# A retention layer and a rational feed-forward on one core: other turns for the first two blocks, sign halfwords on GpSimd, zero products in TensorE's waits

## The chip, the cores and the metric

The kernel runs on one core of a Trainium2 chip. The metric is the device time of one execution in microseconds (us), median of several runs; lower is better. The engines are TensorE (PE; its weight loads are listed as PEld), VectorE (DVE), ScalarE (ACT), GpSimd (POOL) and SyncE (SP), which here only issues DMAs. Each engine works through its own queue in the order written; semaphores make it wait for the others. SBUF is the on-chip memory, PSUM the eight banks (b0 to b7) into which TensorE writes.

## The reference

```
state = gamma[h] * state + k_t (x) v_t           # per batch (4) and head (8), 768 steps, 64 x 64 states
y_t   = (q_t . state) / 8
x     = y as 3072 tokens x 512
h = x @ w_in                                      # 512 -> 2048
P = a0 + a1*h + a2*h^2 + a3*h^3
Q = 1 + |b0|*|h| + |b1|*h^2
out = (P / (Q + 1e-6)) @ w_out                    # 2048 -> 512
```

All inputs are float32, but for `w_in` and `w_out`, which arrive as float64 and must be brought to float32 on the chip.

## The kernel before

**Blocks and slots.** The 768 steps are cut into 6 chunks of 128. Chunk n of the four batches makes block n: 512 tokens. The feed-forward of a block is cut into 16 slices of 128 hidden columns; one slice of one block is a *slot*, 96 in all, numbered k = 0 to 95. The first 32 slots are those of blocks 0 and 1, since the weights are decoded while they run: eight slices of block 0, eight of block 1, the other eight of block 0, the other eight of block 1. Blocks 2 to 5 follow one after the other.

**A slot.** Numbers are split into two parts of lower precision, so each product is three: 12 matmuls of 128x512.
- first product (L665, PSUM tile `ph`): w x, with x in two parts `xh` and `xl`;
- then A1 |h| (L718), A2 scale and offset (L727 on ScalarE, or L723 on GpSimd), A3 (L733), P1 product (GpSimd, L738), D1 (VectorE, L741 and L742), A4 reciprocal (ScalarE, L747 and L750), D2 (VectorE, L754 to L756), A6 cast to `gh` (ScalarE, L762), P2 rest `gl` (GpSimd, L766);
- second product (L680, step O, PSUM tile `po`, banks b4 to b7), which is summed over the slots of a group. Behind a group's last slot four copies (L804) take the sums out; those of the first groups of blocks 0 and 1 go to memory, and are fetched and added (L801) behind the second.

**Decoding a weight tile.** There are 32 tiles of 512 KB (16 of each matrix). `low` (ScalarE, L625) makes the low bits from one byte of each float64, `high` (ScalarE, L629) the high part, VectorE *joins* them in two instructions (L635 shifts and ors the parts, L638 ors the sign bit in), `split` (ScalarE, L644) casts the first part `w[:, 0]`, `rest` (GpSimd, L647) the second. Tile `t`, into which low writes, has two buffers; it is free again after rest.

**Retention.** Chunk c of batch b is *batch* i = 4c + b of 24. It loads kT, qT, v, k (and q2T, v2 for c > 0), GpSimd scales k (L439), TensorE makes scores (S: L312, or L350 and L358), VectorE masks them (L480), TensorE makes the values (R: L318 and L326, or L376), and ScalarE and VectorE write `xh` and `xl` (L569, L573). Batches 0 to 3 make block 0's x; batches 4 to 7, that of block 1, run among the first slots.

**What sets the order.** `Plan` in the kernel orders all steps ahead of time. Each step has engines, a cost, what it follows, the buffers it takes, and a rank, from `RANKS` by batch or tile, or the slot's number, plus an offset by kind (`OFFSETS`). The plan goes through time, and on the engine that can begin first it takes the step of lowest rank that can begin within `LOOK`; A2 goes to whichever of its engines the plan finds (up to slot `SHARED`). `LOADS` ranks the loads. What comes out is the fixed queue of each engine. While TensorE would wait for more than 600 ns ahead of the first first product, `emit` puts in products of a zero tile (L893, tile `idle`).

Of the kernel before, what the change touches and what calls it, by code (L numbers as in the profile page):

```python
# [9 lines left out]
U32 = mybir.dt.uint32  # L10
U8 = mybir.dt.uint8
# [13 lines left out]
COLD = 2600, 3200  # L25
# [19 lines left out]
class Plan:  # L45
# [84 lines left out]
    def order(self, emit):  # L130

        then = {}
        for x in self.steps:
            x.waits = len(x.after)
            for a, _ in x.after:
                then.setdefault(a, []).append(x)
        open_ = []

        def enter(x):
            x.known = 0  # L140
            for a, early in x.after:
                x.known = max(x.known, a.start if early is None else a.end - early + WAKE)
            open_.append(x)

        for x in self.steps:
            if not x.waits:
                enter(x)
        left = len(self.steps)
        while left:
            self.claims = []  # L150
            for x in open_:
                for b in x.takes:
                    if b.options and len(b.options()) == 1:
                        self.claims.append((x, frozenset(b.options()[0])))
            by_engine = {}
            for x in open_:
                t = self.ready(x)
                if t is None:
                    continue
                for e in x.engines:  # L160
# [12 lines left out]
            gap = start - self.free.get(e, 0)  # L173
            self.commit(x, e, start)
            emit(x, e, gap)
            open_.remove(x)
# [8 lines left out]
def tile_retention_rational_ffn(  # L185
# [29 lines left out]
    HF = NF // 2  # L215
# [20 lines left out]
    zeros = ff.tile([P, DM], F32, name="o", bufs=BUFS["o"]).bitcast(BF16)[:, :TB]  # L236
# [171 lines left out]
    def attention(i, rank, load_rank, gate):  # L408
# [38 lines left out]
        pa, aT = Buffer("psum", pairs), [Buffer("aT") for _ in range(2)]  # L447
# [164 lines left out]
    def decode(m, f, rank, load_rank):  # L612
# [8 lines left out]

        def low(_):
            cell["t"] = ff.tile([P, DM], U32, name="t", bufs=BUFS["t"])
            byte = cell["raw"].rearrange("p m w -> p (m w)").bitcast(U8)[:, 3::8]
            nc.scalar.activation(cell["t"], byte, AF.Identity, bias=lcon[:, 0:1], scale=1.0 / 32)  # L625
# [25 lines left out]
        J = step(("DVE",), (1300, 1385), join, [L, U], rank, uses=[t, u], kind="join")  # L651
# [33 lines left out]
    stores, sums, halves = {}, {}, {}  # L685
# [7 lines left out]
    def slot(k, n, f, first, final):  # L693
# [100 lines left out]
        part = None if n >= 2 else f // HF  # L794
        for tt in range(SPB):
            o = Buffer("o") if part != 1 else sums[n, tt][0]

            def copy(engine, tt=tt, o=o):
                if part == 1:
                    o_ = cell["o", tt] = sums[n, tt][1]["tile"]  # L800
# [5 lines left out]
            def write(_, tt=tt):  # L806
                dst = out[(tt * C + n) * P : (tt * C + n + 1) * P, :]
                if part == 0:
                    dst = halves[n, tt] = dram.tile([P, DM], F32, name=f"half{n}_{tt}")
# [3 lines left out]
            after = [(O, early)] + ([sums[n, tt][2]] if part == 1 else [])  # L813
            engines = ("DVE",) if part == 1 else (("ACT",), ("DVE",))[tt % 2]
            Y = step(
                engines, {"ACT": (480, 590), "DVE": (600, 685)}, copy, after, k + 3.6,
                [] if part == 1 else [o], [po] + ([o] if part == 1 else []),
            )
            W = step(("SP",), (ISSUE, 700), write, [Y], k, uses=[o])
            stores[n, part, tt] = W  # L820

    def load_sums(n, gate):
        for tt in range(SPB):
            o = Buffer("o")
            x, cell = load(
                lambda: ff.tile([P, DM], F32, name="o", bufs=BUFS["o"]), lambda tt=tt: halves[n, tt],
                4 * P * DM, 0.0, [o], after=[(gate, None), stores[n, 0, tt]],
# [5 lines left out]
    order = [(n, f) for h in range(2) for n in range(2) for f in range(h * HF, (h + 1) * HF)]  # L833
    order += [(n, f) for n in range(2, NB) for f in range(NF)]
    starts = {}
    for n in range(1, NB):
        end = order.index((n, 0))
        begin = {1: 0, 2: 3 * HF}.get(n, end - NF)
# [3 lines left out]
    with tc.manual_schedule(  # L842
# [25 lines left out]
        for k, (n, f) in enumerate(order):  # L868
# [17 lines left out]
        def emit(x, engine, gap):  # L886

            nonlocal idle
            if engine == "PE" and not begun(1) and gap > 600:
                if idle is None:  # L890
                    idle = ps.tile([P, TB], F32, name="idle", tag="b1")
                for _ in range(min(10, int(gap / 430))):
                    nc.tensor.matmul(idle, zeros[:, :P], zeros, start=True, stop=True)  # L893
            x.run(engine)

# [22 lines left out]
}  # L918
RANKS = {
# [123 lines left out]
```

## Time and profile before

| | |
|---|---|
| median of 3 runs | 621.59 us (620.14 to 621.78) |
| the profiled execution | 622.29 us, of which 620.5 us is the span from the first to the last instruction |
| busy share of the span | PE 97%, DVE 72%, ACT 68%, POOL 56% |
| mean granted TensorE clock | 0.989 |
| DMA | 59.44 MB; HBM read 50.21 MB, written 8.39 MB |

Busy is the time in which at least one instruction of an engine runs. Matmuls are pipelined, so that PE counts as busy while products follow one another; products of zeros count as busy too. The granted clock is the share of full speed that TensorE got. A row of the timeline merges instructions alike in a row: start, duration, engine, line, operation, tiles (out<-in), shapes, count, and in brackets the idle time ahead of it and what ended that.

### The profile page before, as it was taken

Reading aid. Unit: us, or ns where it says so; the run is one execution under the profiler, and the core shown is the slowest. Engines: PE = TensorE matmul, PEld = TensorE weight load, DVE = VectorE, ACT = ScalarE, POOL = GpSimd, SP = SyncE. Lnnn points to the kernel's source line nnn. Section 1 sums busy time; section 2 is a strip of 40 time slices with the busy share of each in tenths; the row PEclk is TensorE's granted clock in tenths of the full one; section 3 lists DMA queues with packets and bytes.
Section 4 is the critical chain, followed back from the end, with each engine's and each line's share of the span. In section 5 each row is a group of like instructions: output and inputs, shape, how many; then the busy total and the mean of one; then the engine's idle time right before and its main releaser. Section 6 shows DMA issues by size and latency. Waiting matters only on the chain.

```text
span 620.5 us, 13030 instructions
## 1 busy us (share of the span) xinstructions
PE 601.5 (97%) x5155; PEld 485.9 (78%) x5155; DVE 449.1 (72%) x743; ACT 421.6 (68%) x700; POOL 347.0 (56%) x303
## 2 busy tenths in 40 slices
PE   8858999999999999999999999999999999999997
PEld 4736877888887888887888888888888888888885
DVE  3689788999979867767766776667766666666662
ACT  1687779999965555565666766666666666776772
POOL 2387677998867675654544545444444444444442
PEclk9968999999999999999999999999999999999999
DMA  8999631003024330224411222112311100100001
GB/s 304 411 414 414 233 86 69 1 1 135 1 86 155 120 120 17 69 69 121 130 43 52 103 73 66 35 52 69 120 52 36 34 1 0 61 9 1 1 0 69
DMA packets 30733, 59.44 MB, mean 96 GB/s; under 512 B 3536, under 2 KB 8912, under 8 KB 30672
## 3 DMA queue, kind: packets, MB, share of 16 engines
q1 hardware_dynamic: 30672, 58.62, 26.8%
q8 instruction: 40, 0.66, 0.4%
q14 instruction: 21, 0.17, 0.1%
HBM read 50.21 MB, written 8.39 MB: 94 GB/s over the span
## 4 chain that ended last, share of the span: by engine, by line
PE 88%; POOL 2%; DVE 1%; ACT 1%; issue 1%; POOLq 0%; DVEq 0%; ACTq 0%
PE po L680 41%; PE ph L665 41%; PE px L376 3%; PE pa L350 2%; PE pa L358 1%; POOL w L647 1%; POOL gl L766 1%; POOL q L738 0%; ACT ph L750 0%; POOL s L723 0%; ACT s L747 0%; DVE q L754 0%; DVE p L756 0%; DVE ph L755 0%; ACT gh L762 0%
## 5 line engine op out<-in xcount | busy, mean ns | idle before, releaser
L665 PE MATMUL ph<-xh,w 128*128 128x512 f32 (+2 forms) x776 | 209.0, 392 | 3.4 <-DVE p L756 2.3
L680 PE MATMUL po<-w,gh 128*128 128x512 f32 x768 | 203.4, 397 | 6.2 <-ACT gh L762 5.3
L738 POOL TENSOR_TENSOR q<-q,s 128x512 f32<-128x512 f32 x96 | 124.2, 1294 | 147.0 <-ACT s L727 144.3
L680 PEld LDWEIGHTS po<-w,gh 128*128 128x128 f32 x768 | 143.0, 189 | 37.6 <-ACT gh L762 5.4
L665 PEld LDWEIGHTS ph<-xh,w 128*128 128x128 f32 x776 | 144.2, 189 | 35.3 <-DVE p L756 4.1
L766 POOL TENSOR_TENSOR gl<-p,gh 128x512 fp32r<-128x512 f32 x96 | 124.1, 1292 | 27.5 <-ACT gh L762 18.0
L754 DVE SCALAR_TENSOR_TENSOR q<-q,small,ph 128x512 f32<-128x512 f32 x96 | 71.6, 745 | 93.7 <-ACT ph L750 91.8
L718 ACT ACTIVATE q<-ph 128x512 f32<-128x512 f32 x96 | 57.3, 596 | 87.7 <-PE ph L665 87.3
L680 PE MATMUL po<-w,gl 128*128 128x512 f32 x384 | 111.6, 392 | 0.9 <-POOL gl L766 0.9
L665 PE MATMUL ph<-xl,w 128*128 128x512 f32 (+2 forms) x388 | 104.0, 390 | 0.0
L747 ACT ACTIVATE s<-q,small 128x512 f32<-128x512 f32 x96 | 69.5, 724 | 49.2 <-POOL q L738 49.2
L741 DVE TENSOR_TENSOR p<-ph,p 128x512 f32<-128x512 f32 x96 | 65.8, 685 | 30.2 <-ACT p L733 29.1
L680 PEld LDWEIGHTS po<-w,gl 128*128 128x128 f32 x384 | 72.6, 189 | 16.8 <-POOL gl L766 1.7
L665 PEld LDWEIGHTS ph<-xl,w 128*128 128x128 f32 x388 | 73.2, 189 | 15.3
L733 ACT ACTIVATE p<-ph,small 128x512 f32<-128x512 f32 x96 | 74.3, 774 | 2.1 <-POOL gl L766 2.1
L742 DVE SCALAR_TENSOR_TENSOR p<-p,small,ph 128x512 f32<-128x512 f32 x96 | 71.8, 748 | 3.4
L762 ACT CAST gh<-p 128x512 fp32r<-128x512 f32 x96 | 59.2, 617 | 20.1 <-PE po L680 13.0
L755 DVE SCALAR_TENSOR_TENSOR ph<-p,small,ph 128x512 f32<-128x512 f32 x96 | 71.9, 749 | 0.0
L756 DVE SCALAR_TENSOR_TENSOR p<-q,ph 128x512 f32<-128x512 f32 x96 | 65.9, 686 | 3.3
L750 ACT ACTIVATE ph<-s 128x512 f32<-128x512 f32 x96 | 57.8, 602 | 3.7
L647 POOL TENSOR_TENSOR w<-t,w 128x512 fp32r<-128x512 f32 x32 | 41.2, 1293 | 19.8 <-ACT w L644 10.8
L727 ACT ACTIVATE s<-q,small 128x512 f32<-128x512 f32 x61 | 49.7, 814 | 0.3
(53 smaller groups left out, 445.8 us busy)
## 6 DMA issues: line engine op xcount, KB each, us to landing
raw<-in_w_in SPq DMA_DIRECT2D x16, 512.0 KB, 7.6
raw<-in_w_out SPq DMA_DIRECT2D x16, 512.0 KB, 7.8
kT<-in_kT SPq DMA_DIRECT2D x24, 256.0 KB, 3.3
qT<-in_qT SPq DMA_DIRECT2D x24, 256.0 KB, 3.2
v<-in_v SPq DMA_DIRECT2D x24, 256.0 KB, 3.9
k<-in_k SPq DMA_DIRECT2D x24, 256.0 KB, 3.6
out<-o SPq DMA_DIRECT2D x24, 256.0 KB, 2.6
q2T<-in_q2T SPq DMA_DIRECT2D x20, 128.0 KB, 3.2
```

Of the source, the lines that this page charges most:

```text
L665: nc.tensor.matmul(cell["ph"][:, t0:t1], w[0, f][:, part, kt * P : (kt + 1) * P], x[:, kt, t0:t1], start=(i == 0), stop=(i == 3 * NP - 1),)
L680: nc.tensor.matmul(o_tiles[n][tt], g_[:, tt * P : (tt + 1) * P], w[1, f][:, part], start=(first and m == 0), stop=(last and m == 2),)
L733: nc.scalar.activation(cell["p"], cell["ph"], AF.Identity, bias=par_sb[:, 2:3], scale=par_sb[:, 3:4])
L738: nc.gpsimd.tensor_mul(cell["q"], cell["q"], cell["s"])
L741: nc.vector.tensor_mul(cell["p"], cell["ph"], cell["p"])
L742: nc.vector.scalar_tensor_tensor(cell["p"], cell["p"], par_sb[:, 1:2], cell["ph"], ALU.add, ALU.mult)
L747: nc.scalar.activation(cell["s"], cell["q"], AF.Abs_reciprocal_sqrt, bias=qcon[:, 0:1])
L754: nc.vector.scalar_tensor_tensor(q_, q_, qcon[:, 0:1], ph_, ALU.add, ALU.mult)
L755: nc.vector.scalar_tensor_tensor(ph_, p_, par_sb[:, 0:1], ph_, ALU.add, ALU.mult)
L756: nc.vector.scalar_tensor_tensor(p_, q_, 2.0, ph_, ALU.subtract, ALU.mult, reverse0=True)
L762: nc.scalar.copy(cell["gh"], cell["p"])
L766: nc.gpsimd.tensor_sub(cell["gl"], cell["p"], cell["gh"].bitcast(F32))
```

## The change

- `GROUPS = (0, 10, 16)`: the first 32 slots go in groups of 10, 10, 6 and 6 instead of four of 8.
- For 14 of the 32 weight tiles (`SIGNS`) GpSimd makes the upper halfword of `t`, which holds only the sign, with one compare-and-multiply on 16-bit elements; `low` then writes the lower halfword alone, and one VectorE instruction joins (L638 goes).
- Products of zeros (`fill`, 37 in all; 23 before) now also stand in waits of over 900 ns behind the first first product, into the bank that the next step takes or, as a sum of zeros, into the open sum of a second product. The zeros have a tile of their own.
- `t` has three buffers. The masked scores of batches 0 to 3 take buffers of `o`. The last of the four copies is ScalarE's and the first VectorE's.
- The plan's constants (`COLD`, `HOLD`, `LOOK`, `EARLY`, `SHARED`), ranks, offsets and load ranks are others; the plan looks only at the six loads of lowest rank.

```
-COLD = 2600, 3200
+COLD = 2600, 1000
...
+    def fill(bank, start):
+        for _ in range(spare[0]):
+            nc.tensor.matmul(
+                bank, zeros, zeros.unsqueeze(1).broadcast_to([P, TB // P, P]), start=start, stop=start,
+                skip_group_check=True,
+            )
+        spare[0] = 0
...
+        aside = (m, f) in SIGNS
         def low(_):
...
-            nc.scalar.activation(cell["t"], byte, AF.Identity, bias=lcon[:, 0:1], scale=1.0 / 32)
+            to = cell["t"].bitcast(U16)[:, ::2] if aside else cell["t"]
+            nc.scalar.activation(to, byte, AF.Identity, bias=lcon[:, 0:1], scale=1.0 / 32)
+
+        def sign(_):
+            words = cell["raw"].rearrange("p m w -> p (m w)").bitcast(U16)[:, 3::4]
+            nc.gpsimd.tensor_scalar(
+                cell["t"].bitcast(U16)[:, 1::2], words, 32768.0, 32768.0, op0=ALU.is_ge, op1=ALU.mult
+            )
...
         def join(_):
             u_, t_ = cell["u"], cell["t"]
+            if aside:
+                nc.vector.scalar_tensor_tensor(
+                    t_, u_, 3, t_, ALU.logical_shift_left, ALU.bitwise_or
+                )
+                return
...
-        J = step(("DVE",), (1300, 1385), join, [L, U], rank, uses=[t, u], kind="join")
+        N = aside and step(("POOL",), (780, 820), sign, [L], rank, uses=[t], kind="sign")
+        J = step(
+            ("DVE",), (650, 735) if aside else (1300, 1385), join, [L, U, N], rank, uses=[t, u], kind="join"
+        )
...
-    order = [(n, f) for h in range(2) for n in range(2) for f in range(h * HF, (h + 1) * HF)]
+    order = [(n, f) for a, b in zip(GROUPS, GROUPS[1:]) for n in range(2) for f in range(a, b)]
...
-            if engine == "PE" and not begun(1) and gap > 600:
-                if idle is None:
-                    idle = ps.tile([P, TB], F32, name="idle", tag="b1")
-                for _ in range(min(10, int(gap / 430))):
-                    nc.tensor.matmul(idle, zeros[:, :P], zeros, start=True, stop=True)
+            if engine == "PE" and gap > 900:
+                spare[0] = min(12, int(gap / FILL))
+                if not begun(1):
+                    if idle is None:
+                        idle = ps.tile([P, TB], F32, name="idle", tag="b1")
+                    fill(idle, True)
+                elif open_po:
+                    fill(open_po[0], False)
             x.run(engine)
+            spare[0] = 0
...
-HOLD = 1500
+HOLD = 3000
+FILL = 400
+SIGNS = ((1, 0), (0, 1), (0, 4), (1, 5), (1, 6), (1, 7), (0, 8), (0, 9), (0, 10), (0, 13), (1, 13), (0, 14), (1, 14), (0, 15))
+GROUPS = (0, 10, 16)
 BUFS = {
-    "gh": 3, "gl": 3, "o": 4, "t": 2, "p": 2, "q": 2, "s": 2,
+    "gh": 3, "gl": 3, "o": 4, "t": 3, "p": 2, "q": 2, "s": 2,
...
-    0: -7.706, 1: 0.948, 2: -14.342, 3: -8.309, 4: 1.673, 5: 5.071, 6: 2.038, 7: 4.242,
+    0: -12.58, 1: -4.475, 2: -8.957, 3: -16.343, 4: 0.239, 5: -6.099, 6: 6.639, 7: 19.176,
...
-LOOK = {"ACT": 50, "DVE": 50, "POOL": 100}
-EARLY = 3
-SHARED = 40
+LOOK = {"ACT": 50, "DVE": 0, "POOL": 200}
+EARLY = 4
+SHARED = 30
```

TensorE's queue, before, from slot 0's first product (cut into 384 and 128 columns) on; `pa` are the scores of batch 4:

```order
L665 MATMUL ph<-xh,w 128x384 x4
L665 MATMUL ph<-xl,w 128x384 x4
L665 MATMUL ph<-xh,w 128x384 x4
L350 MATMUL pa<-qT,kT 64x64 x16
L358 MATMUL pa<-v,k 64x64 x16
L665 MATMUL ph<-xh,w 128x128 x4
L665 MATMUL ph<-xl,w 128x128 x4
L665 MATMUL ph<-xh,w 128x128 x4
L665 MATMUL ph<-xh,w 128x512 x4
L665 MATMUL ph<-xl,w 128x512 x4
L665 MATMUL ph<-xh,w 128x512 x4
```

The same place now; `pk` are the first states of all four batches:

```order
L702 MATMUL ph<-xh,w 128x384 x4
L702 MATMUL ph<-xl,w 128x384 x4
L702 MATMUL ph<-xh,w 128x384 x4
L354 MATMUL pk<-v,k 64x64 x32
L702 MATMUL ph<-xh,w 128x128 x4
L702 MATMUL ph<-xl,w 128x128 x4
L702 MATMUL ph<-xh,w 128x128 x4
L702 MATMUL ph<-xh,w 128x512 x4
L702 MATMUL ph<-xl,w 128x512 x4
L702 MATMUL ph<-xh,w 128x512 x4
L280 LDWEIGHTS zeros
L280 MATMUL pa<-zeros 128x512
```

The first states, which stood among batches 0 to 3, stand inside slot 0's first product, and batch 4's scores come behind slot 1's, after 11 zero products. The first products of slots 2 and 3 now stand ahead of slot 0's second product, too; before, only slot 1's did. At the other end, before, the first products of slots 0 to 11 and the second ones of slots 0 to 9 end with slot 9's second product, and they do so now.

GpSimd's queue, before, from the first scaling of k on:

```order
L439 TENSOR_TENSOR k<-k,small 128x512 x4
L647 TENSOR_TENSOR w<-t,w 128x512
L439 TENSOR_TENSOR k<-k,small 128x512
L647 TENSOR_TENSOR w<-t,w 128x512 x2
L723 TENSOR_SCALAR s<-q,small 128x512
L738 TENSOR_TENSOR q<-q,s 128x512
L533 TENSOR_TENSOR state<-after,small 128x256
```

The same now (L681 is rest, L457 the scaling of k, L652 the sign, L768 A2 and L783 P1):

```order
L681 TENSOR_TENSOR w<-t,w 128x512
L457 TENSOR_TENSOR k<-k,small 128x512 x4
L652 TENSOR_SCALAR t<-raw 128x512
L681 TENSOR_TENSOR w<-t,w 128x512
L768 TENSOR_SCALAR s<-q,small 128x512
L783 TENSOR_TENSOR q<-q,s 128x512
L681 TENSOR_TENSOR w<-t,w 128x512
```

The first rest now stands ahead of the scalings of k, and a sign ahead of the second rest; 14 signs are in the queue in all, and 17 A2 instead of 35 (ScalarE has 79 instead of 61).

VectorE's queue, before, from the first join on:

```order
L635 SCALAR_TENSOR_TENSOR u<-u,t 128x512
L638 SCALAR_TENSOR_TENSOR t<-raw,u 128x512
L573 TENSOR_TENSOR xl<-px,xh 128x2x128 x2
L635 SCALAR_TENSOR_TENSOR u<-u,t 128x512
L638 SCALAR_TENSOR_TENSOR t<-raw,u 128x512
```

And now:

```order
L669 SCALAR_TENSOR_TENSOR u<-u,t 128x512
L672 SCALAR_TENSOR_TENSOR t<-raw,u 128x512
L499 TENSOR_TENSOR aT<-pa,first 128x384 x2
L593 TENSOR_TENSOR xl<-px,xh 128x2x128 x2
L499 TENSOR_TENSOR aT<-pa,first 128x384 x2
L593 TENSOR_TENSOR xl<-px,xh 128x2x128 x4
L665 SCALAR_TENSOR_TENSOR t<-u,t 128x512
```

The first weight tile is joined ahead of the masks of batches 2 and 3 instead of behind them, and the second in one instruction (L665 of the new code).

More of the change, by code (lines that the diff above doesn't have):

```diff
@@ L1 @@
+import bisect
 from contextlib import ExitStack
@@ L10 @@
 U32 = mybir.dt.uint32
+U16 = mybir.dt.uint16
 U8 = mybir.dt.uint8
@@ L136, in order @@
                 then.setdefault(a, []).append(x)
-        open_ = []
+        open_, loads = [], []
         def enter(x):
@@ L142, in enter @@
                 x.known = max(x.known, a.start if early is None else a.end - early + WAKE)
-            open_.append(x)
+            if x.engines == ("SP",):
+                bisect.insort(loads, x, key=lambda y: y.rank)
+            else:
+                open_.append(x)
         for x in self.steps:
@@ L154, in order @@
                         self.claims.append((x, frozenset(b.options()[0])))
-            by_engine = {}
-            for x in open_:
+            by_engine, some = {}, 0
+            for x in open_ + loads:
+                if some == 6:
+                    break
                 t = self.ready(x)
@@ L159, in order @@
                     continue
+                some += x.engines == ("SP",)
                 for e in x.engines:
@@ L175, in order @@
             emit(x, e, gap)
-            open_.remove(x)
+            (loads if e == "SP" else open_).remove(x)
             left -= 1
@@ L235, in tile_retention_rational_ffn @@
     state = const.tile([P, B, NP, D], F32, name="state")
-    zeros = ff.tile([P, DM], F32, name="o", bufs=BUFS["o"]).bitcast(BF16)[:, :TB]
+    zeros = const.tile([P, P], BF16, name="zeros")
     wp = ctx.enter_context(tc.tile_pool(name="wp", bufs=1))
@@ L266, in pairs @@
         return [names[i : i + 2] for i in range(0, len(names) - 1, 2)]
+    open_po, spare = [], [0]
+    def fill(bank, start):
[5 more added lines that the diff above has]
+        spare[0] = 0
     def load(dst, src, nbytes, rank, takes=(), uses=(), after=()):
@@ L445, in attention @@
         )
-        pa, aT = Buffer("psum", pairs), [Buffer("aT") for _ in range(2)]
+        pa, aT = Buffer("psum", pairs), [Buffer("aT" if c else "o") for _ in range(2)]
         before = bursts.get(i - 2 if i < B else i - 1)
@@ L452, in run_scores @@
             banks = [psum(pa, s, "pa") for s in range(2)]
+            fill(banks[0], True)
             if c:
@@ L673, in gemm_out @@
             o_tiles[n] = [psum(po, i, "po") for i in range(SPB)]
+            fill(o_tiles[n][0], True)
+        open_po[:] = [] if last else [o_tiles[n][0]]
         terms = ((cell["gh"], 0), (cell["gh"], 1), (cell["gl"], 0))
@@ L683, in gemm_out, with group_of @@
             )
-    stores, sums, halves = {}, {}, {}
+    stores, sums, parts = {}, {}, {}
+    def group_of(n, f):
+        return sum(f >= x for x in GROUPS[1:]) if n < 2 else 0
     def turn(name, x):
@@ L793, in slot @@
             return
-        part = None if n >= 2 else f // HF
+        g = group_of(n, f)
+        early_sum, late_sum = n < 2 and g > 0, n < 2 and g < len(GROUPS) - 2
         for tt in range(SPB):
-            o = Buffer("o") if part != 1 else sums[n, tt][0]
+            o = sums[n, tt][0] if early_sum else Buffer("o")
             def copy(engine, tt=tt, o=o):
-                if part == 1:
-                    o_ = cell["o", tt] = sums[n, tt][1]["tile"]
+                if early_sum:
+                    o_ = cell["o", tt] = cell["sums"][tt]["tile"]
                     nc.vector.tensor_add(o_, o_tiles[n][tt], o_)
@@ L807, in write @@
                 dst = out[(tt * C + n) * P : (tt * C + n + 1) * P, :]
-                if part == 0:
-                    dst = halves[n, tt] = dram.tile([P, DM], F32, name=f"half{n}_{tt}")
+                if late_sum:
+                    dst = parts[n, tt] = dram.tile([P, DM], F32, name=f"part{n}_{g}_{tt}")
                 nc.sync.dma_start(out=dst, in_=cell["o", tt])
             early = (3 - tt) * 3 * 227
-            after = [(O, early)] + ([sums[n, tt][2]] if part == 1 else [])
-            engines = ("DVE",) if part == 1 else (("ACT",), ("DVE",))[tt % 2]
+            after = [(O, early)] + ([sums[n, tt][2]] if early_sum else [])
+            engines = ("DVE",) if early_sum else (("DVE",), ("ACT",))[tt % 2]
             Y = step(
                 engines, {"ACT": (480, 590), "DVE": (600, 685)}, copy, after, k + 3.6,
-                [] if part == 1 else [o], [po] + ([o] if part == 1 else []),
+                [] if early_sum else [o], [po] + ([o] if early_sum else []),
             )
             W = step(("SP",), (ISSUE, 700), write, [Y], k, uses=[o])
-            stores[n, part, tt] = W
+            stores[n, tt] = W
+        if early_sum:
+            cell["sums"] = [sums[n, tt][1] for tt in range(SPB)]
     def load_sums(n, gate):
@@ L825, in load_sums @@
             x, cell = load(
-                lambda: ff.tile([P, DM], F32, name="o", bufs=BUFS["o"]), lambda tt=tt: halves[n, tt],
-                4 * P * DM, 0.0, [o], after=[(gate, None), stores[n, 0, tt]],
+                lambda: ff.tile([P, DM], F32, name="o", bufs=BUFS["o"]), lambda tt=tt: parts[n, tt],
+                4 * P * DM, 0.0, [o], after=[(gate, None), stores[n, tt]],
             )
             sums[n, tt] = o, cell, x
-    order = [(n, f) for h in range(2) for n in range(2) for f in range(h * HF, (h + 1) * HF)]
+    order = [(n, f) for a, b in zip(GROUPS, GROUPS[1:]) for n in range(2) for f in range(a, b)]
     order += [(n, f) for n in range(2, NB) for f in range(NF)]
@@ L837, in tile_retention_rational_ffn @@
         end = order.index((n, 0))
-        begin = {1: 0, 2: 3 * HF}.get(n, end - NF)
+        begin = {1: 0, 2: order.index((0, NF - 1)) + 1}.get(n, end - NF)
         for a in range(B):
@@ L877, in tile_retention_rational_ffn @@
                 built += 1
-            first = f == 0 or (n < 2 and f == HF)
-            last = f == NF - 1 or (n < 2 and f == HF - 1)
-            if n < 2 and f == NF - 1:
+            first = f in (GROUPS if n < 2 else (0,))
+            last = f + 1 in (GROUPS if n < 2 else (NF,))
+            if last and group_of(n, f):
                 load_sums(n, gemms_out[-2])
```

13 lines of the change are left out of this document (7 added, 6 removed), and 45 rows, old and new, of tables (LOADS, OFFSETS, RANKS).

## The prediction

> **What bounds the kernel now.** I read the page's head and its chain first, then busy time by stage, then TensorE's timeline.
>
> ```profile
> span 620.5 us, 13030 instructions
> PE 601.5 (97%) x5155; PEld 485.9 (78%) x5155; DVE 449.1 (72%) x743; ACT 421.6 (68%) x700; POOL 347.0 (56%) x303
> PE 88%; POOL 2%; DVE 1%; ACT 1%; issue 1%; POOLq 0%; DVEq 0%; ACTq 0%
> ```
>
> TensorE carries the chain, but 97% is a mean over stages. By stage (length, then busy us and count of PE, PEld, DVE, ACT, POOL, then granted clock, DMA share, GB/s):
>
> ```profile
> 37.20:44.00 6.80, 5.85 (x13) 3.72 (x14) 6.43 (x11) 5.67 (x10) 4.43 (x4) 0.50 1.04 414
> 44.00:58.00 14.00, 11.32 (x166) 8.92 (x165) 11.25 (x22) 11.79 (x21) 10.78 (x11) 0.99 1.03 414
> 58.00:66.00 8.00, 8.00 (x72) 6.32 (x76) 5.96 (x9) 5.68 (x11) 4.84 (x5) 0.79 1.03 419
> 66.00:95.40 29.40, 28.19 (x323) 21.87 (x313) 24.59 (x44) 22.38 (x40) 21.15 (x21) 1.00 0.35 112
> 108.20:157.00 48.80, 48.79 (x215) 40.09 (x214) 45.15 (x68) 46.32 (x79) 43.62 (x38) 1.00 0.12 44
> 157.00:616.40 459.40, 459.35 (x3823) 374.93 (x3821) 321.87 (x530) 298.74 (x489) 237.33 (x203) 1.00 0.18 58
> ```
>
> From 108.2 to 616.4 TensorE is busy 508.14 of 508.20 us at full clock: only less work on it would help there, and the change takes none away. What can be won lies ahead, where it waits and twice runs at a lower clock (0.50, 0.79). Its timeline there (start, duration; in brackets the gap and what ended it):
>
> ```profile
> 20.67 1.25 PE L893 MATMUL idle<-o 128*128 128x512 bf16 x5
> 23.02 0.98 PE L665 MATMUL ph<-xh,w 128*128 128x384 f32 x4 [1.10 <-ACT w L644]
> ...
> 37.21 1.22 PE L680 MATMUL po<-w,gh 128*128 128x512 f32 x2 [5.27 <-ACT gh L762]
> 39.37 0.80 PE L680 MATMUL po<-w,gl 128*128 128x512 f32 x1 [0.94 <-POOL gl L766]
> ...
> 45.09 0.63 PE L350 MATMUL pa<-qT,kT 64*64 64x64 f32 x27 [0.68 <-DVE t L638]
> ...
> 57.97 2.05 PE L665 MATMUL ph<-xh,w 128*128 128x512 f32 x4 [2.00 <-DVE p L756]
> ...
> 78.77 0.99 PE L350 MATMUL pa<-qT,kT 64*64 64x64 f32 x29
> ...
> 80.22 1.19 PE L665 MATMUL ph<-xh,w 128*128 128x512 f32 x4
> ...
> 95.40 1.19 PE L680 MATMUL po<-w,gh 128*128 128x512 f32 x4 [0.90 <-POOL w L647]
> ...
> 108.22 1.98 PE L680 MATMUL po<-w,gh 128*128 128x512 f32 x8
> ...
> 110.94 1.07 PE L665 MATMUL ph<-xh,w 128*128 128x512 f32 x4
> ```
>
> A pass, one first or second product of a slot, is 12 matmuls: 108.22 to 110.94, 2.72 us. At 110.94 TensorE has done the first products of slots 0 to 11, the second ones of slots 0 to 9 and batches 0 to 7. I call that the mark. In the new order the second product of slot 9 again ends 22 passes and the same eight batches, so 170 passes, 16 batches and the tail stay behind it, unchanged: the change is worth what it moves the mark by, plus any gap that it opens behind. From 23.02 to the mark are 87.9 us. Work in it: 22 x 2.72 = 59.8, and four batches of about 2.5 (the scores of one, 78.77 to 80.22, are 1.45): 10, together 70. So 18 us are lost: 9.8 in the gaps shown, 2.9 at half clock (half of 5.85), 1.7 at 0.79 (0.21 of 8.00); the other 3.5 are slot 0's cut pass, smaller gaps and changes of tiling.
>
> **The change, part by part.** *Turns after ten slots, new ranks.* Block 1 is wanted two slots later, but ten slots need 20 decoded weight tiles where eight needed 16. Counted in the order up to what slot 9's second product needs: VectorE 20 joins against 17 and no copies against 2; ScalarE 21 low, 21 high and 20 splits against 18, 18 and 17, 2 scalings (A2) against 3, no copies against 2; GpSimd 20 rests against 17, 9 A2 against 8, and 8 signs. The prices:
>
> ```profile
> L638 DVE SCALAR_TENSOR_TENSOR t<-raw,u 128x512 uint32<-128x512 uint32 x32 | 22.0, 688 | 2.2
> L804 DVE COPY o<-po 128x512 f32<-128x512 f32 x12 | 8.2, 686 | 6.7 <-PE po L680 6.7
> L625 ACT ACTIVATE t<-raw,small 128x512 uint32<-128x512 uint8 x32 | 24.2, 763 | 4.3 <-POOL w L647 3.9 <-DMA raw<-in_w_in 0.4
> L629 ACT ACTIVATE u<-raw 128x512 f32<-128x512 f32 x32 | 20.1, 635 | 0.0
> L644 ACT CAST w<-t 128x512 fp32r<-128x512 f32 x32 | 19.8, 618 | 3.2 <-DVE t L638 2.8 <-ACT u L629 0.3
> L727 ACT ACTIVATE s<-q,small 128x512 f32<-128x512 f32 x61 | 49.7, 814 | 0.3
> L804 ACT COPY o<-po 128x512 f32<-128x512 f32 x12 | 7.1, 590 | 6.7 <-PE po L680 6.7
> L647 POOL TENSOR_TENSOR w<-t,w 128x512 fp32r<-128x512 f32 x32 | 41.2, 1293 | 19.8 <-ACT w L644 10.8 <-DMA v<-in_v 8.8
> L723 POOL TENSOR_SCALAR s<-q,small 128x512 f32<-128x512 f32 x35 | 27.0, 772 | 39.9 <-ACT q L718 35.1 <-DVE p L756 4.8
> ```
>
> *The sign halfword.* Where it is used, the second join goes (L638, 0.69 us), 8 times in the first ten slots and 14 in all, 9.6 us of VectorE. GpSimd gets a one-input operation on 16-bit elements read 8 bytes apart. No row shows that. Nearest is its one-input row L723, 0.77; the other end is the two-input rows, 1.29, doubled for compare and multiply, 2.59. Below 0.77 nothing speaks for it. I take 0.77: same engine, one input, two operations, 512 elements. The sign waits for low, and queued behind it on GpSimd are rests and the P1 of the running slot.
>
> Sums to slot 9: VectorE -1.4 for copies, +3 x 1.38 - 8 x 0.69 for joins = -2.7 us. ScalarE +3 x 2.02 - 0.81 - 1.18 = +4.1. GpSimd +3.9 + 0.8 + 8 x 0.77 = +10.8. Their ends in this trace, for slot 9:
>
> ```profile
> 103.70 0.69 DVE L756 SCALAR_TENSOR_TENSOR p<-q,ph 128x512 f32<-128x512 f32 x1
> ...
> 104.42 0.62 ACT L762 CAST gh<-p 128x512 fp32r<-128x512 f32 x1
> ...
> 106.85 1.29 POOL L766 TENSOR_TENSOR gl<-p,gh 128x512 fp32r<-128x512 f32 x1
> ```
>
> *Loads.* The first weight tile is issued before batch 2 now, no longer behind 5 MB of other loads. What the first product then waits for last is batch 3's data: 4.1 MB into the queue instead of the tile's 5.1. At 414 GB/s 1.0 MB is 2.4 us, so it starts at about 20.6. The far end of the queue is unchanged: batch 7's values are issued behind all 32 weight tiles (SP's timeline).
>
> ```profile
> 70.95 1.92 SPq L275 DMA_DIRECT2D v<-in_v  x2
> ...
> v<-in_v SPq DMA_DIRECT2D x24, 256.0 KB, 3.9
> ```
>
> Such a load lands 3.9 us after its issue (second row, the page's DMA issues), so batch 7's scores can't begin before 75; they began at 78.77.
>
> *Three t buffers.* They end ScalarE's waits for GpSimd's rests, the second row here (waits up to 108 us: total, times, longest). They free ScalarE, not TensorE itself.
>
> ```profile
> ACT q L718 <- PE ph L665: 5.1, 5, 2.0
> ACT t L625 <- POOL w L647: 3.6, 5, 0.9
> ```
>
> *Zero products.* 37 instead of 23; of the new order 19 stand ahead of the first weight product, 11 before batch 4's scores, 3 before slot 2's first product, 4 before batch 7's scores. At the 0.21 us of 20.67's five, the 18 are 3.8 us; at half clock, twice that. They stand in waits like the 5.27 and 2.00 above, so I cost them at nothing; without that cover they cost the 3.8. They win at most the 4.6 us of low clock. The trace's warning: the clock was halved behind a gap of only 2.00 us. The Trainium skill (TensorE: Matmul & The Clock Gate, Why this matters for your kernels) says that gaps up to about 3 us keep the clock; the 57.97 row differs. By the page the remaining short gaps would cost no clock and the sum would be up to 1.7 us lower; I go by the row.
>
> *The sum for the mark.* Three floors. TensorE: 20.6 + 70 = 90.6. Loads: scores of batch 7 at 75, then 1.45, eight passes (21.8) and 1.1 for its values: 99.3. VectorE: 104.4 - 2.7 for work - 2.4 for the earlier start = 99.3, then 0.6 for the cast and a pass: 102.6. ScalarE is the unsure one: 105.0 + 4.1 - 2.4 = 106.7 if it waits as much as now, 98.0 if the 3.6 and 5.1 of the waits above both go. Half of them gives 102.4, and a pass later 105.1. GpSimd has room: its window 66.00:95.40 is 72% busy. I take 104 between VectorE's and ScalarE's result: 6.9 us earlier. Ends: 99.3 (11.6 earlier) and 109.4 (1.5 earlier).
>
> *Behind the mark.* Slots 10 to 19: ScalarE has four A2 more, two low and one high less, +1.1 us; it stood at 46.32 of 48.80, so at about 97% of the 54.4 us that ten slots take on TensorE. GpSimd gets 6 signs for 4 A2: from 89% to 92%. It fits, with nothing to spare; between 0 and 3 us, I take 0.3. Later slots: 79 A2 on ScalarE instead of 61, in a stage where it is 65% busy: nothing. The order of products, two to four slots apart, and the tail's four copies are of the same kinds: nothing.
>
> Sum: 6.9 - 0.3 = 6.6 us. The profiled execution took 622.29 (span 620.5), so 615.7; the runs' median is 621.59, 0.7 lower, so **615.0**.
>
> **Rivals.** (1) *ScalarE eats it.* For: every sum above gives it more, and it has the fullest row from 108.20. Against: it idled 7.0 us in 66.00:95.40. With its waits unchanged the mark comes at 109.4, and up to 3 us are lost behind it: 620.1 to 623. (2) *Slower: the sign costs GpSimd 2.59.* Between slots 9 and 19 it would have 6 x 1.82 = 10.9 us more on top of 92% of 54.4: 7 us too many, which TensorE waits for, and the mark gains nothing: 628. It decides from about 1.5 us a sign. Against it: L723's 0.77. (3) *Zero products in the way.* If the operands come earlier than the gaps were meant, TensorE finishes 18 products first: 3.8 us, 618.8. (4) *The floors are reached:* mark at 99.3, 610.
>
> **How the numbers follow.** Forecast 0.58, rival 4 0.10, rival 3 0.06, rival 1 0.17, rival 2 0.09. A measurement of this kernel tells about 0.3% from no change, 1.9 us: faster is below 619.7. Faster: the forecast, 4, 3 and a little of 1: 0.76; same 0.12 and slower 0.12 from 1 and 2. The range goes from the load floor less one us for its rounding (609) to 621.5, which holds half of rival 1.
>
> **What would show it.** Right: the second product of slot 9 ending near 104; the clock at 1.00 from 30 to 66; no TensorE gap behind the mark; signs near 0.77; joins alone at 0.69. Wrong: waits of TensorE for gh (ScalarE) between 105 and 160, signs above 1.5, or half clock between 30 and 60 all the same.

## The result, and the profile after

The changed kernel takes 627.67 us (median of 4 runs, 625.65 to 627.95) against 621.54 before (620.14 to 621.78): ratio 1.0096, 95% interval 1.007 to 1.0122. It is 6.1 us slower; 6.6 us faster was forecast. The profiled execution took 627.9 us.

The page of the changed kernel, its head and its chain:

```profile
span 626.1 us, 12983 instructions
...
PE 607.7 (97%) x5169; PEld 487.1 (78%) x5169; DVE 444.4 (71%) x729; ACT 438.7 (70%) x718; POOL 361.6 (58%) x299
...
PE 75%; POOL 15%; DMA 3%; issue 2%; ACT 2%; SPq 1%; DVE 1%; POOLq 0%; DVEq 0%; ACTq 0%
```

TensorE is as "busy" as before (97%) and GpSimd only 2 points busier, but GpSimd's share of the chain went from 2% to 15%. The groups of the decoding (last columns: busy us, mean ns; then idle time ahead and who ended it) say with what:

```profile
L652 POOL TENSOR_SCALAR t<-raw 128x512 uint16<-128x512 uint16 x14 | 29.7, 2128 | 0.1
...
L648 ACT ACTIVATE t<-raw,small 128x512 uint32<-128x512 uint8 x18 | 13.8, 766 | 1.2 <-DVE aT L499 1.0 <-POOL w L681 0.2
L648 ACT ACTIVATE t<-raw,small 128x512 uint16<-128x512 uint8 x14 | 12.2, 882 | 1.9 <-POOL w L681 1.3 <-DMA raw<-in_w_in 0.6
L665 DVE SCALAR_TENSOR_TENSOR t<-u,t 128x512 uint32<-128x512 uint32 x14 | 9.5, 687 | 7.0 <-POOL t L652 6.5 <-ACT u L658 0.4
```

One sign takes 2.13 us, not 0.77, and VectorE's single join then waits for it (6.5 us in all). The joins themselves are the forecast 0.69. Low into halfwords takes 0.12 us more than into words.

By stage (length, busy us and count of PE, PEld, DVE, ACT, POOL, then granted clock, DMA share, GB/s):

```profile
23.00:44.00 21.00, 16.18 (x176) 10.83 (x175) 15.04 (x27) 17.80 (x30) 19.17 (x16) 0.77 0.92 368
80.00:108.00 28.00, 24.68 (x215) 18.43 (x214) 20.48 (x35) 22.08 (x39) 26.15 (x23) 0.94 0.20 60
108.20:157.00 48.80, 47.06 (x206) 37.76 (x205) 39.70 (x59) 46.10 (x78) 46.95 (x37) 1.00 0.06 22
...
180.00:622.00 442.00, 441.83 (x3746) 360.61 (x3744) 310.52 (x506) 296.47 (x476) 212.06 (x176) 1.00 0.19 60
```

From 108.20 to 157.00 GpSimd is busy 46.95 of 48.80 us: it is the full engine there, and TensorE loses 1.74 us where it lost 0.01 before. From 180 on TensorE is busy all through, as before. TensorE's timeline:

```profile
18.08 0.97 PE L702 MATMUL ph<-xh,w 128*128 128x384 f32 x4
...
32.13 0.69 PE L376 MATMUL pa<-v,k 64*64 64x64 f32 x32 [2.20 <-POOL k L457]
32.76 0.82 PE L280 MATMUL ph<-zeros 128*128 128x512 bf16 x3
35.13 2.07 PE L702 MATMUL ph<-xh,w 128*128 128x512 f32 x4 [1.55 <-ACT w L678]
...
39.97 2.08 PE L702 MATMUL ph<-xh,w 128*128 128x512 f32 x4 [1.06 <-POOL w L681]
...
84.59 0.69 PE L376 MATMUL pa<-v,k 64*64 64x64 f32 x32 [2.32 <-POOL k L457]
85.22 1.89 PE L702 MATMUL ph<-xh,w 128*128 128x512 f32 x4
...
111.98 1.07 PE L702 MATMUL ph<-xh,w 128*128 128x512 f32 x4
...
129.09 1.20 PE L702 MATMUL ph<-xh,w 128*128 128x512 f32 x4 [0.58 <-DVE p L801]
...
141.63 1.19 PE L702 MATMUL ph<-xh,w 128*128 128x512 f32 x4 [1.16 <-DVE p L801]
...
165.58 1.21 PE L702 MATMUL ph<-xh,w 128*128 128x512 f32 x4 [1.19 <-DVE p L801]
```

The first weight product starts at 18.08, 4.9 us earlier than before. By the mark, which is at 111.98, all of it is gone: TensorE waited for GpSimd's scaled k (2.20 and 2.32) and rest (1.06) and for ScalarE's split (1.55), and four matmuls take 1.9 to 2.1 us where the clock is halved, 1.1 to 1.2 elsewhere. The mark is 1.04 us later than before's 110.94. The last matmul ends at 622.03, 510.05 behind the mark; before it was 616.35, 505.41 behind (the last row of TensorE's timeline, before and now):

```profile
615.96 0.39 PE L680 MATMUL po<-w,gl 128*128 128x512 f32 x1
...
621.64 0.39 PE L719 MATMUL po<-w,gl 128*128 128x512 f32 x1
```

So 4.6 us more are lost behind it, 2.9 of them in the three gaps shown. These read "<-DVE p", but the cause is on GpSimd. Around the second of them, GpSimd's timeline, with a row of ScalarE and one of VectorE:

```profile
132.07 2.14 POOL L652 TENSOR_SCALAR t<-raw 128x512 uint16<-128x512 uint16 x1
...
133.69 0.81 ACT L772 ACTIVATE s<-q,small 128x512 f32<-128x512 f32 x1
...
134.12 2.57 POOL L681 TENSOR_TENSOR w<-t,w 128x512 fp32r<-128x512 f32 x2
...
136.64 1.31 POOL L783 TENSOR_TENSOR q<-q,s 128x512 f32<-128x512 f32 x1
...
140.89 0.69 DVE L801 SCALAR_TENSOR_TENSOR p<-q,ph 128x512 f32<-128x512 f32 x1
```

The P1 of the running slot (L783) stands behind a sign and two rests, back to back. Its input s is there at 134.50, when A2 (L772) ends, but P1 begins 2.1 us later. A4 and D2 (L801), on other engines, follow P1, and TensorE's next first product, at 141.63, needs the bank that D2 frees at 141.58.

### The profile page after: what moved, and what is told of

It is laid out like the page before. It is cut to its first block, busy times and chain, and to the rows that moved or that the text cites. A ratio compares the mean times of both kernels' runs of the same rounds, so it can differ in the third digit from the quotient of the medians.

```text
span 626.1 us, 12983 instructions
## 1 busy us (share of the span) xinstructions
PE 607.7 (97%) x5169; PEld 487.1 (78%) x5169; DVE 444.4 (71%) x729; ACT 438.7 (70%) x718; POOL 361.6 (58%) x299
## 4 chain that ended last, share of the span: by engine, by line
PE 75%; POOL 15%; DMA 3%; issue 2%; ACT 2%; SPq 1%; DVE 1%; POOLq 0%; DVEq 0%; ACTq 0%
PE ph L702 35%; PE po L719 34%; POOL w L681 4%; POOL t L652 4%; PE px L394 3%; POOL q L783 3%; POOL gl L811 3%; PE pa L368 2%; PE pa L376 1%; POOL s L768 1%; SPq L293 1%; DMA v<-in_v 1%; DMA raw<-in_w_out 1%; DMA k<-in_k 1%; POOL k L457 0%
## 5 line engine op out<-in xcount | busy, mean ns | idle before, releaser
L783 POOL TENSOR_TENSOR q<-q,s 128x512 f32<-128x512 f32 x96 | 124.8, 1300 | 184.7 <-ACT s L772 183.4
L702 PE MATMUL ph<-xh,w 128*128 128x512 f32 (+2 forms) x776 | 212.1, 395 | 5.8 <-DVE p L801 2.9
L792 ACT ACTIVATE s<-q,small 128x512 f32<-128x512 f32 x96 | 69.6, 725 | 34.2 <-POOL q L783 33.9
L801 DVE SCALAR_TENSOR_TENSOR p<-q,ph 128x512 f32<-128x512 f32 x96 | 65.9, 687 | 3.3
L772 ACT ACTIVATE s<-q,small 128x512 f32<-128x512 f32 x79 | 64.5, 817 | 2.3
L681 POOL TENSOR_TENSOR w<-t,w 128x512 fp32r<-128x512 f32 x32 | 41.1, 1297 | 18.7 <-ACT w L678 18.7
```

The source lines that it names most:

```text
L681: nc.gpsimd.tensor_sub(w[m, f][:, 1], cell["t"].bitcast(F32), w[m, f][:, 0].bitcast(F32))
L702: nc.tensor.matmul(cell["ph"][:, t0:t1], w[0, f][:, part, kt * P : (kt + 1) * P], x[:, kt, t0:t1], start=(i == 0), stop=(i == 3 * NP - 1),)
L783: nc.gpsimd.tensor_mul(cell["q"], cell["q"], cell["s"])
L792: nc.scalar.activation(cell["s"], cell["q"], AF.Abs_reciprocal_sqrt, bias=qcon[:, 0:1])
L801: nc.vector.scalar_tensor_tensor(p_, q_, 2.0, ph_, ALU.subtract, ALU.mult, reverse0=True)
```

## The experiments

**Which part of the sign costs?** A kernel of its own with forms of GpSimd's one-input operation and of low, four of each. `words` are the upper halfwords of the float64s and `half` those of a 32-bit tile, both on every fourth or second 16-bit element; `hi` is the upper word; `f` and `te` are float32 without gaps.

```
+ nc.gpsimd.tensor_scalar(half, words, 32768.0, 32768.0, op0=ALU.is_ge, op1=ALU.mult)   # L47
+ nc.gpsimd.tensor_scalar(half, hi.bitcast(F32), -(2.0 ** 30), 32768.0, op0=ALU.mult, op1=ALU.min)   # L55
+ nc.gpsimd.tensor_scalar(te, f, 0.0, 32768.0, op0=ALU.is_lt, op1=ALU.mult)             # L59
+ nc.gpsimd.tensor_scalar(half, words, 2.0, 3.0, op0=ALU.mult, op1=ALU.add)             # L63
+ nc.gpsimd.tensor_scalar(half[:, :128], words[:, :128], 32768.0, 32768.0, op0=ALU.is_ge, op1=ALU.mult)   # L65
```

> Ten forms of GpSimd's tensor_scalar and two of ScalarE's low, four of each in a row, nothing else on the engine. Theory 1 (compare on 16-bit integers is what costs): the sign's own form 2.1 us, the same on contiguous operands also about 2.1, mult and add on the same 16-bit operands clearly less, float32 mult and add 0.77, and 128 instead of 512 elements about 0.6. Theory 2 (the strided reads and writes cost): contiguous operands 0.8, and float32 read 8 bytes apart well above 0.77. Low into halfwords 0.88 against 0.77 into words.

Groups of that run by form:

```profile
L55 POOL TENSOR_SCALAR ta<-raw 128x512 uint16<-128x512 f32 x4 | 8.3, 2082 | 0.0
...
L47 POOL TENSOR_SCALAR ta<-raw 128x512 uint16<-128x512 uint16 x4 | 8.3, 2078 | 0.0
...
L59 POOL TENSOR_SCALAR te<-f 128x512 f32<-128x512 f32 x4 | 7.7, 1921 | 1.6 <-DVE c L35 1.6
...
L63 POOL TENSOR_SCALAR ta<-raw 128x512 uint16<-128x512 uint16 x4 | 3.0, 762 | 0.3
L65 POOL TENSOR_SCALAR ta<-raw 128x128 uint16<-128x128 uint16 x4 | 2.7, 683 | 0.3
```

L47 and L63 have the same input and output and differ in the two operations (and their constants): 2.08 us for compare-and-multiply, 0.76 for multiply-and-add. Float32 without gaps and with a compare (L59) takes 1.92. So the 16-bit type and the stride are not what costs, and theory 2 is out. Theory 1 had the compare right, but its type too narrow, and multiply-and-minimum (L55) is as slow without any compare. The price grows with the elements: (2078 - 683) / 384 = 3.6 ns each, worked out from these two lengths.

**A cheap sign, and the same order.** The sign on 128 of 512 columns (the signs of the others are left out), low in whole words; every queue keeps its order.

```
- cell["t"].bitcast(U16)[:, 1::2], words, 32768.0, 32768.0, op0=ALU.is_ge, op1=ALU.mult
+ cell["t"].bitcast(U16)[:, 1:256:2], words[:, :P], 32768.0, 32768.0, op0=ALU.is_ge, op1=ALU.mult
```

> The changed kernel with every queue in the same order, but the sign made for 128 of 512 columns only, and low written as whole words (0.77 instead of 0.88); the signs of the other columns are left out. Theory 1 (the sign's 2.13 us on GpSimd is the loss): 14 signs of about 0.6 give back some 21 us of GpSimd, no gaps behind the mark, the mark 6 to 9 us earlier: 612 to 617. Rival A (ScalarE and the order of the products are the loss): no more than 2 us, 625 to 627.

613.92 us (612.89 to 614.81), ratio to before 0.9885 (0.9867 to 0.9904), with the sign at

```profile
L652 POOL TENSOR_SCALAR t<-raw 128x128 uint16<-128x128 uint16 x14 | 9.7, 698 | 0.9 <-ACT t L648 0.9
```

At about the price that the prediction took, the time is 1.1 us from the forecast. It does not yet tell the sign from low's whole words.

**No signs at all.** `SIGNS` empty, ranks as they are; the plan orders all queues anew.

```
- SIGNS = ((1, 0), (0, 1), (0, 4), ...
+ SIGNS = ()
```

> The changed kernel with an empty list of signs (every tile joined in two instructions), so that the plan orders it anew with the same ranks. Theory 1: GpSimd is free again, VectorE has 9.6 us more; 614 to 620. Rival A: 624 to 628, since ScalarE's queue is as long as in the changed kernel.

639.85 us (638.51 to 641.75), ratio 1.03 (1.027 to 1.0331): a miss for every expectation, and no measure of the signs. In the new order a slot's chain comes too late, and TensorE's timeline has

```profile
124.09 5.28 PE L280 MATMUL ph<-zeros 128*128 128x512 bf16 x12 [6.62 <-DVE p L801]
```

a gap of 6.62 us, then twelve zero products at half clock (5.28 us) in the way. The ranks found with signs did not carry over to the steps without them; all later runs of the whole kernel but one keep the order.

**No zero products behind the first first product**, 18 of them.

```
-                elif open_po:
-                    fill(open_po[0], False)
+                else:
+                    spare[0] = 0
```

> The changed kernel without the 18 zero products behind the first weight product; otherwise the same queues. Theory 1: they stand in waits for GpSimd and the clock is halved all the same, so within 1 us of 627.7. Rival B (they stand in the way): 3 to 4 us faster. If they did save clock: 2 to 5 us slower.

626.63 us (626.39 to 627.32), ratio to before 1.0092 (1.0077 to 1.0107); the changed kernel has 1.0096. The zero products neither cost nor bring anything measurable here: the clock was halved with them and is halved without them.

**The sign by two additions**, all columns, same order.

```
- words, 32768.0, 32768.0, op0=ALU.is_ge, op1=ALU.mult
+ words, 2.0 ** 38 - 16384, 2.0 ** 38, op0=ALU.add, op1=ALU.subtract
```

> The changed kernel with the sign made by two additions instead of a comparison and a multiplication: 2^38 - 16384 is added, which rounds to a multiple of 32768, and 2^38 taken off; the result is 0 or 32768 as before, on all 512 columns, and the order of every queue is the same. Theory 1 (the 2.13 us of the comparison on GpSimd is the whole loss): the sign's row at about 0.76 us, as multiply-and-add took in the run of forms; GpSimd no longer back to back between 113 and 168 us; mark near 104; 613 to 616.5 us, that is 0.5 us or so above the run with narrow signs for low's dearer write of halfwords (14 x 0.12 us on ScalarE). Rival A (the gain of the narrow signs came from low in whole words on ScalarE): 619 to 624 us with the sign at 0.76 all the same. Rival B (GpSimd's cost lies in rounding to 16 bits whatever the operation): sign at 2.1 us, 627 us.

631.31 us (630.82 to 631.8), ratio 1.0162 (1.0146 to 1.0178), with 2.12 us a sign. The expected 0.76 was wrong: addition and subtraction are as dear as the compare. It is slower than the changed kernel although the row is the same. In the traces the operation behind a sign starts 2.06 us after the sign did in the changed kernel (33.28 to 35.34) and 2.20 here (34.66 to 36.86); 14 times that is 2.0 us. In the profiled executions the mark is 1.5 us later than in the changed kernel (113.47), and 1.4 us more are lost behind it. What makes up the rest stays open.

**The same without zero products** (the two edits together).

> The run with additions without the 18 zero products behind the first first product. With the dear sign, leaving them out made no difference (626.6 against 627.7 us), but there the clock was halved in spite of them. Theory 1 (they cost nothing and keep little): within 1.5 us of the run with additions, mean granted clock at most 0.01 lower. Rival (with a cheap sign the waits are short enough that they keep the clock): 2 to 5 us more than the run with additions, with a stretch of 3.4 or 10 us at half clock between 25 and 65 us.

631.62 us (629.59 to 631.99), ratio 1.0161 (1.0139 to 1.0183): the same as with them. Since the sign was still dear, it only repeats the run without zero products.

**The sign on 384 columns** (the others' signs are left out, low in whole words, same order): a price between.

```
+ cell["t"].bitcast(U16)[:, 1:768:2], words[:, : 3 * P], 32768.0, 32768.0, op0=ALU.is_ge, op1=ALU.mult
```

> The changed kernel with signs on 384 of 512 columns (the other columns' signs are left out, and low writes whole words), same order of every queue. The sign should take about 0.22 + 384 x 0.00363 = 1.61 us. If there is a threshold at about 1.5 us a sign, as the prediction said (GpSimd's room covers what is below it): 614 to 618 us, most of GpSimd's waits between 113 and 168 us gone. Rival (no threshold, since every sign stands ahead of its join and split whatever room there is on average): on the line between 0.70 us a sign (613.9 us) and 2.13 (627.7): 621 to 624 us.

620.47 us (619.67 to 622.14), ratio 0.9991 (0.9978 to 1.0004): between the two expectations. The sign took

```profile
L652 POOL TENSOR_SCALAR t<-raw 128x384 uint16<-128x384 uint16 x14 | 23.0, 1649 | 0.9 <-ACT t L648 0.9
```

and TensorE's timeline shows three waits, at full clock all through (1.2 us for four matmuls):

```profile
31.03 0.69 PE L376 MATMUL pa<-v,k 64*64 64x64 f32 x32 [1.94 <-POOL k L457]
...
33.90 1.20 PE L702 MATMUL ph<-xh,w 128*128 128x512 f32 x4 [1.42 <-ACT w L678]
...
37.94 1.20 PE L702 MATMUL ph<-xh,w 128*128 128x512 f32 x4 [1.92 <-POOL w L681]
```

Its mark is at 106.61, and the last matmul ends 507.19 behind it.

**The plan told the true prices** of sign and low; all queues ordered anew.

```
-        L = step(("ACT",), (651, 761), low, [got], rank, [t], kind="low")
-        N = aside and step(("POOL",), (780, 820), sign, [L], rank, uses=[t], kind="sign")
+        L = step(("ACT",), (770, 882) if aside else (651, 761), low, [got], rank, [t], kind="low")
+        N = aside and step(("POOL",), (2070, 2126), sign, [L], rank, uses=[t], kind="sign")
```

> The changed kernel with the plan told what sign and low really take (2.07 to 2.13 us and 0.77 to 0.88), so that it orders all queues anew with the same ranks; 89 A2 go to ScalarE. Theory 1 (the loss is GpSimd's work itself, 14 x 1.36 us too much ahead of and among ten slots that need it): no order mends much of it, and ranks found for other prices fit badly, as in the run without signs: 622 to 640 us. Rival C (the loss is an order made for wrong prices, which a right one mends): 613 to 618 us.

645.16 us (644.48 to 645.58), ratio 1.0384 (1.0367 to 1.0401), worse than either expectation. As in the run without signs, a new order with old ranks loses more than anything under test; the worst stage is

```profile
120.00:140.00 20.00, 14.61 (x55) 9.72 (x54) 11.25 (x17) 14.68 (x25) 16.46 (x14) 0.83 0.00 1
```

Right prices alone did not mend the order; what the plan could do with new ranks at this price is left open.

**Which pairs of operations are short?** A second kernel of forms, all on 16-bit elements 8 bytes apart: L53 multiply-add in bfloat16, L55 add-subtract, L57 multiply alone, L61 multiply-multiply, L65 multiply-subtract, L67 add-multiply (and five more).

```
+ nc.gpsimd.tensor_scalar(bhalf, bwords, 0.0, -0.0, op0=ALU.mult, op1=ALU.add)             # L53
+ nc.gpsimd.tensor_scalar(half, words, 2.0 ** 38, 2.0 ** 38, op0=ALU.add, op1=ALU.subtract)   # L55
+ nc.gpsimd.tensor_scalar(half, words, 1.0, None, op0=ALU.mult)                            # L57
```

> Forms of GpSimd's one-input operation alone, four of each, all on 16-bit elements 8 bytes apart, 512 of them. So far multiply-and-add took 0.61 to 0.76 us, and compare-and-multiply, multiply-and-minimum and add-and-subtract 1.92 to 2.13. Theory 1' (multiply followed by add is the only short pair): multiply-and-add and its bfloat16 form (times 0, plus -0) at 0.76 us; add-subtract, add-add, multiply-multiply, multiply-subtract and add-multiply at 2.1. Rival (only the first operation counts, multiply being short): multiply-multiply and multiply-subtract at 0.76 too. Single operations and the copy: 1.0 or less if each operation is a pass of its own, 2.1 if all but multiply-and-add are the slow kind.

```profile
L55 POOL TENSOR_SCALAR ta<-raw 128x512 uint16<-128x512 uint16 x4 | 8.4, 2090 | 0.3
...
L65 POOL TENSOR_SCALAR ta<-raw 128x512 uint16<-128x512 uint16 x4 | 8.3, 2087 | 0.3
L57 POOL TENSOR_SCALAR ta<-raw 128x512 uint16<-128x512 uint16 x4 | 6.6, 1654 | 0.3
...
L67 POOL TENSOR_SCALAR ta<-raw 128x512 uint16<-128x512 uint16 x4 | 3.0, 760 | 0.3
L61 POOL TENSOR_SCALAR ta<-raw 128x512 uint16<-128x512 uint16 x4 | 3.0, 760 | 0.3
...
L53 POOL TENSOR_SCALAR ta<-raw 128x512 bf16<-128x512 bf16 x4 | 3.0, 760 | 0.3
```

Neither expectation fits. Short are multiply-add, multiply-multiply and add-multiply (0.76 us, as a copy); long are multiply-subtract, add-subtract and add-add (2.09); one operation alone, multiply or compare, takes 1.65. L61, L65 and L67 have the same two constants (1.0 and 1.0), so it is the operations that decide, not the numbers. Why is not seen in a trace; that it is so, is enough to make a cheap sign.

**The sign by multiply-and-add**, all 512 columns, same order: the upper halfword is read as bfloat16, times 0, plus -0, which leaves the sign bit alone.

```
- cell["t"].bitcast(U16)[:, 1::2], words, 32768.0, 32768.0, op0=ALU.is_ge, op1=ALU.mult
+ cell["t"].bitcast(BF16)[:, 1::2], words, 0.0, -0.0, op0=ALU.mult, op1=ALU.add
```

> The changed kernel, whose sign is now made by multiply-and-add: the upper halfword of each float64 is read as a bfloat16, multiplied by 0 and -0 is added, so that +0 or -0 is left, which is the sign alone; on all 512 columns, same order of every queue. Theory 1 (the 2.13 us on GpSimd is the whole loss): the sign's row at 0.76 us, mark near 102 to 103, no wait of TensorE for GpSimd over 0.5 us behind it; 613 to 616 us, that is faster than both kernels. Rival A (part of the narrow signs' gain came from low in whole words): 617 to 620 us with the sign at 0.76.

614.57 us (613.53 to 615.48), ratio 0.9892 (0.9873 to 0.9911): faster than both kernels. Its sign, its stages and TensorE's timeline:

```profile
L652 POOL TENSOR_SCALAR t<-raw 128x512 bf16<-128x512 bf16 x14 | 11.0, 791 | 0.1
```

```profile
23.00:44.00 21.00, 17.67 (x195) 12.47 (x195) 18.70 (x33) 20.51 (x37) 19.66 (x20) 1.00 1.04 411
80.00:108.00 28.00, 27.18 (x177) 21.65 (x176) 25.32 (x41) 26.81 (x48) 24.31 (x23) 1.00 0.20 67
108.20:157.00 48.80, 48.80 (x215) 39.95 (x214) 40.12 (x60) 46.63 (x79) 43.53 (x38) 1.00 0.01 2
```

```profile
17.70 0.97 PE L702 MATMUL ph<-xh,w 128*128 128x384 f32 x4
...
30.87 0.69 PE L376 MATMUL pa<-v,k 64*64 64x64 f32 x32 [1.50 <-POOL k L457]
31.50 0.82 PE L280 MATMUL ph<-zeros 128*128 128x512 bf16 x3
33.83 1.20 PE L702 MATMUL ph<-xh,w 128*128 128x512 f32 x4 [1.51 <-ACT w L678]
...
102.03 1.07 PE L702 MATMUL ph<-xh,w 128*128 128x512 f32 x4
...
607.28 0.39 PE L719 MATMUL po<-w,gl 128*128 128x512 f32 x1
```

Full clock in all three stages, TensorE busy all through the third, and the mark at 102.03. Low still writes halfwords here, so the 13.1 us between this run and the changed kernel are the sign's operation alone.

**The same without zero products** behind the first first product.

> The run before without the 18 zero products behind the first first product. With dear signs they were worth nothing (626.6 us without, 627.7 with; 631.6 and 631.3 with additions). In the run with 384 columns the clock stayed full through waits of 1.9, 1.4 and 1.9 us with zero products ahead of them, where the kernel before lost it behind a bare 2.0 us. Theory 2 (zero products keep the clock once the rest of each wait is below 2 us): half clock for 3.4 to 10 us between 28 and 45 us, mean granted clock 0.990 to 0.995, 1.7 to 5 us more than with them. Rival (they do nothing): within 1 us, clock as with them.

615.14 us (614.76 to 615.99), ratio 0.9906 (0.9889 to 0.9923). TensorE's waits are longer, and work runs at half the clock behind them,

```profile
31.08 1.13 PE L376 MATMUL pa<-v,k 64*64 64x64 f32 x32 [3.87 <-POOL k L457]
34.05 2.07 PE L702 MATMUL ph<-xh,w 128*128 128x512 f32 x4 [1.84 <-ACT w L678]
```

as theory 2 had it, but the time changes by 0.6 us only, where it expected 1.7 to 5; each ratio lies inside the other's interval. In the profiled executions the last matmul ends 1.2 us later. So the zero products do keep the clock here, but for little: TensorE has to wait for its operands there anyway.

## Why the prediction was wrong, step by step

- **The price of a sign: the step that failed.** "I take 0.77: same engine, one input, two operations, 512 elements" chose the nearest row by engine and shape. What decides is which two operations: L723 multiplies and adds. The sign took 2.13 us. The other end that the prediction named, 2.59, was nearer.
- **Rival 2 came true, and was given 0.09.** It said 628, with no gain at the mark and 7 us lost behind it; measured are 627.67, 1.0 lost at the mark and 4.6 behind it. Its mechanism holds, but that its number is met to 0.3 us is luck: it took 2.59 us a sign. By its own sum with the measured 2.13 (6 x 1.36 us on top of 92% of 54.4) GpSimd has 3.8 us too many behind the mark; in those 54.4 us it was busy all but 0.4, and 4.6 were lost. The mark, which it took as unmoved, came later.
- **Its threshold of "about 1.5 us a sign" was too high.** At 1.65 us 5.9 of the 6.6 us are already gone (620.47 against 614.57). If every us of extra GpSimd work (14 x the difference) cost one from some price on, that price would be 1.65 - 5.9 / 14, an estimate of 1.2 us; no run has a price between 0.79 and 1.65. With 384 columns the mark comes 4.6 us later than with the cheap sign, and 1.5 more are lost behind it. So most of the loss is ahead of the mark, where the prediction said that GpSimd has room by the 72% of one window.
- **The rest of the sum came out as a total, in part by luck.** With the sign at 0.79 us the time is 614.57 where 615.0 was forecast; against its own comparison's 621.22 it is 6.65 us faster, against 6.6. Its parts were less exact. The first weight product starts at 17.70 instead of the forecast 20.6: the scores of the fourth batch begin 2.1 us earlier (14.68; 16.79 before), near the forecast 2.4, but the first product follows them in 3.0 us instead of 6.2, since the split of the first tile ends at 14.4 and no longer at 23.0. The mark is at 102.03, beyond the forecast 104, near the VectorE result of 102.6. The last matmul ends 607.67 - 102.03 = 505.64 behind the mark, 0.2 us more than before; 0.3 was taken. The mark came 8.9 us earlier, where 6.9 was forecast, and the medians still differ by 6.65 only: the profiled execution of before (622.29) lies 0.7 above its median and that of the cheap sign (613.53) 1.0 below its own.
- **Fullness behind the mark:** ScalarE 46.63 of 48.80 us (96%; 97% forecast), GpSimd 43.53 (89%; 92% forecast) with the cheap sign. Rivals 1 and 4 did not come: TensorE has no wait for `gh` there, and the mark stayed above the loads' 99.3.
- **Zero products at nothing:** right, by 626.63 against 627.67 and 615.14 against 614.57. Rival 3 showed only in the two orders made anew (5.28 us of zero products at half clock without signs, 4.85 with true prices).
- **The clock.** The prediction went by the row that lost the clock behind 2.00 us. The runs side with the row: in the changed kernel the clock was halved behind one gap of 2.32 us and behind 2.20 followed by 1.55, and it stayed full through 1.94, 1.42 and 1.92 with 384 columns. The Trainium skill (TensorE: Matmul & The Clock Gate, Why this matters for your kernels) gives gaps of about 3 us as what to stay below; here 2.32 us was too long, and 1.94 was not.
- **Where the changed kernel lost its early start.** Up to the mark its profiled execution is 9.95 us behind that with the cheap sign: 0.4 in the start, 3.9 in gaps of TensorE (8.3 against 4.4 us in all that its timeline lists), and the rest fits the half clock. In slices of 1 us the clock is 0.5 from 34.3 to 44.5 and from 85.5 to 88.9; without the idle time in them that is 11.7 us of work at half speed, an estimate of 5.8 us lost. With 384 columns the gaps add up to 8.9 us, at full clock. So between 1.65 and 2.13 us a sign, what these executions lose more ahead of the mark is clock, not waiting.

## What to carry to other kernels

Price a new instruction by a row that has the same operations, not only the same engine, inputs and shape; where none has, both ends belong in the forecast with like chances, or the form is measured alone first. Judge an engine's room by the stage and by what stands behind the new step in its queue: GpSimd was 58% busy over the whole changed kernel, and its signs still held up steps that TensorE waited for. An order found for one set of prices is part of the kernel: both orders made anew with the old ranks were slower here, so change a price inside it and keep the order, or search again.

## What the runs showed that I had not expected

- GpSimd's two-scalar operation on 512 elements takes 0.61 to 0.76 us for multiply-add, multiply-multiply and add-multiply, 1.92 to 2.13 for compare-multiply, multiply-minimum, add-add, add-subtract and multiply-subtract, and 1.65 for a multiply or a compare alone: one operation can take longer than two.
- A sign bit can be had from multiply-and-add: a bfloat16 times 0 plus -0, 0.79 us in the kernel.
- ScalarE's low takes 0.88 us into every second halfword and 0.77 into words.
- Telling the plan the truth about two steps made the kernel 17.5 us slower (645.16 against 627.67).
